# A strided 1-D convolution with norm and GELU, forward and backward: paired sums joined, and pair sums of four combinations kept off the raw step buffers

## The chip, the cores and the metric

The kernel runs on one core of a Trainium2 chip. The metric is device time in microseconds (us) of one launch, inputs and outputs in device memory. A core has a matrix engine (TensorE, PE in the profile, with PEld for its weight loads), a vector engine (VectorE, DVE), a scalar engine (ScalarE, ACT), GpSimd (POOL), and SyncE (SP), whose queue issues the DMA transfers here. Each engine takes its own instructions in their order; semaphores tie the engines together.

## The reference

A convolution of 31 taps and stride 2 over 2 x 16000 steps of 256 channels, a normalisation over time per channel, GELU, and the gradients of all four inputs.

```python
def _fwd_reference(x, w, gn_gamma, gn_beta):
    B, T, D = x.shape            # 2, 16000, 256
    K = w.shape[0]               # 31
    s = 2
    L = (T - K) // s + 1         # 7985
    h = jnp.einsum('blc,cd->bld', x[:, 0:s * L:s, :], w[0])
    for i in range(1, K):
        h = h + jnp.einsum('blc,cd->bld', x[:, i:i + s * L:s, :], w[i])
    mu = jnp.einsum('bld->bd', h)[:, None, :] / L
    var = jnp.einsum('bld->bd', (h - mu) ** 2)[:, None, :] / L
    h = (h - mu) / jnp.sqrt(var + 1e-5)
    h = h * gn_gamma[None, None, :] + gn_beta[None, None, :]
    return _gelu(h)

def reference(x, w, gn_gamma, gn_beta, grad_out):
    out, vjp = jax.vjp(_fwd_reference, x, w, gn_gamma, gn_beta)
    return (out, *vjp(grad_out))
```

## The kernel before

**Stages.** F0 and F1 are the forward convolution of the two batches, in four chunks each (`forward`); G0 and G1 the gradient with respect to x (`input_grad`); W the gradient of the weights (`weight_grad`). Normalisation and GELU (`gelu_batch`) of a batch run beside the stage that follows its convolution.

**Fewer products, more sums.** A convolution over an index of two values is computed with three products in place of four: one with the first operand (called `A`), one with the second (`C_`), and one with a sum or difference (`B_`). This is done on several index levels, so that matmuls are traded for sums of bf16 data on DVE. In the forward stages `f_sums` makes them: `first` level sums for a branch, `second` (for the leaves `A` and `C_`) and `third`, each over `F = 1088` columns and, as a rule, for both parities of a step. The sums for parity 0 take `o[:, 0]` and `o[:, 1]` in place; those for parity 1 take `o[:, 1]` and `o[:, 0]` one column on. So they are two instructions, of 1088 and 1087 columns (the helper `tt`, L561). In the input gradient `g_sums` does the same with 258 and 257 columns for two channel halves (L1121). `f_three_ac` and `g_three_ac` use the two halves of a `third` sum in separate groups of matmuls, `f_three_b` and `f_outer` the product with weight differences (`w_sub`, L551), whose results ACT copies with both signs.

**The weight gradient.** `weight_grad` goes through nine combinations n = 0 to 8 of two indices, in the order `COMBOS`: (A,A), (A,C_), (A,B_), (C_,B_), (B_,B_), (B_,A), (B_,C_), (C_,A), (C_,C_). Each needs four tiles of x (`x_tile`, one for each of two batches and two values of a third index) and two of gradient differences (`d_tile`). A tile of x is one raw load for n = 0, 1, 7, 8; two raw loads that DVE adds (`w_add`, L1413) for n = 3, 5, 6; and for n = 2 and 4 a sum of tiles that are there. The second raw load of a tile goes to one of two buffers `XR`, at bytes 57344 and 65536 of the arena. In each combination DVE makes pair sums of x (`pair_x`, L1508) and pair differences of the gradient (`pair_d`, L1516, two instructions of 1024 elements, one for each of two places around a middle one); PE makes their products (`w_pairs`, `w_single`), `w_both` (L1540) puts two partial results into one accumulator, and `leaf_d` (L1587) makes differences along the last index. `pair_x` and `pair_d` write to a set of buffers that `place(n)` picks in turn from those that n allows: "all" is always there, "early" for n below 2, and "late", which starts at byte 57344 and so lies on both `XR`, for all n but 3 and 5. After combination 3, `w_done` spills four partial results (`pcd`) to memory, and combination 7 loads them back.

**The order of the instructions** isn't that of the program. `Plan` collects every operation with its engine, an estimated duration and the cells of memory that it touches. `Plan.order` gives each a due time from what needs it, from `slack` and a table `lead` (an offset for each kind of operation and stage), and `Plan.listing` then lists the operations engine by engine, the earliest due first among those ready; `look` is how far PE may reach ahead, `pads` what is allowed for around a DMA, `PACE` how the GELU units are spread over a stage, and `plan.hold` keeps what was recorded under it back until PE has come so far. The program is emitted in that order, so that each engine's queue is fixed at build time. `w2_part` prepares transposed weights for the input gradient, a quarter in each chunk of F0.

## Time and profile before

| | us |
|---|---|
| median of 3 runs | 1187.01 |
| lowest and highest | 1183.07 and 1188.23 |
| the profiled execution, its own time | 1189.54 |
| its span | 1187.8 |
| PE busy | 1149.0 |
| DVE busy | 1047.6 |
| ACT busy | 570.0 |

The profile is one execution. The page gives for each engine the busy time, its share of the span and the number of instructions; the stretches give the busy time of each engine in a window, with the clock granted to TensorE (1.00 is full) and the mean busy share of the DMA engines; the groups give a line, engine, operation, shapes and count, then busy time, mean ns of one instruction, idle time ahead of them and what ended it. Rows in order of time begin with the start and the length in us, and end with the idle time ahead of them and its releaser in brackets. By the rows of PE, the forward stages end near 428 us, the input gradient near 861 us, and the weight gradient takes the rest.

### The profile page before, as it was taken

The page shows a single profiled execution, that of the slowest core. Times are in us where ns is not written, and L with a number is a line of the kernel's source. Part 1 is how long each engine was busy: PE and PEld are TensorE (multiplying, and loading weights), DVE is VectorE, ACT ScalarE, POOL GpSimd, SP SyncE. Part 2 cuts the span into 40 slices and gives each one's busy share as a digit, 9 for nine tenths or more (in the row PEclk, how much of TensorE's full clock was granted, in tenths as well). Part 3 has the DMA queues.
Part 4 walks back from the last instruction along what each step waited for, and adds up shares of the span by engine and source line. Part 5 has one row for each costly group of instructions (what it writes and reads, how often), then busy time and mean ns, then how long its engine had stood idle before and what let it go on. Part 6 is the DMA issues. An engine that isn't in the chain of part 4 may idle for free.

```text
span 1187.8 us, 19338 instructions
## 1 busy us (share of the span) xinstructions
PE 1149.0 (97%) x7739; PEld 763.5 (64%) x7796; DVE 1047.6 (88%) x1358; ACT 570.0 (48%) x873; POOL 18.9 (2%) x67
## 2 busy tenths in 40 slices
PE   5999999999999999999999999999999999989998
PEld 3888889777777964444444444444488656656685
DVE  7997898799999989999879997788889898777995
ACT  1254454788885578978884476433322212111200
POOL 0000000000000000000000000000000000000000
PEclk9999999999999999999999999999999999999999
DMA  9446949968986799567639998697998824986774
GB/s 212 73 115 122 200 121 182 205 146 204 204 209 124 270 353 252 167 225 186 221 115 292 270 329 265 161 318 266 317 235 266 271 90 151 359 300 198 239 219 140
DMA packets 334100, 255.17 MB, mean 215 GB/s; under 512 B 187500, under 2 KB 312682, under 8 KB 325738
## 3 DMA queue, kind: packets, MB, share of 16 engines
q1 hardware_dynamic: 333818, 253.93, 76.6%
q8 instruction: 61, 1.00, 0.3%
q14 instruction: 29, 0.24, 0.1%
q0 software_dynamic: 192, 0.00, 0.0%
HBM read 118.95 MB, written 89.62 MB: 176 GB/s over the span
## 4 chain that ended last, share of the span: by engine, by line
PE 46%; DVE 14%; DMA 6%; issue 4%; ACT 1%; SPq 0%; DVEq 0%; ACTq 0%
PE ps L1162 27%; PE ps L1447 15%; PE ps L596 4%; DVE arena L1413 3%; DMA arena<-in_x_dram 2%; DMA arena<-dnd 2%; DVE arena L1357 2%; DVE arena L1587 2%; DVE ps L676 1%; DVE arena L676 1%; DVE arena L1516 1%; DVE arena L1508 1%; DMA dnd<-arena 1%; DVE arena L1121 1%; DVE ps L1540 1%
## 5 line engine op out<-in xcount | busy, mean ns | idle before, releaser
L1162 PE MATMUL ps<-arena 128*128 128x512 bf16 x1974 | 429.7, 376 | 6.6 <-DVE ps L676 3.6
L596 PE MATMUL ps<-arena 128*128 128x256 bf16 (+4 forms) x3460 | 408.2, 281 | 17.8 <-DVE arena L551 7.1
L596 PEld LDWEIGHTS <-arena 128*128 128x128 bf16 x3460 | 338.1, 99 | 87.7 <-DVE arena L551 7.5
L1162 PEld LDWEIGHTS <-arena 128*128 128x128 bf16 x2016 | 197.3, 98 | 237.7 <-issue 6.8
L1447 PE MATMUL ps<-arena 128*128 128x256 bf16 (+1 forms) x2305 | 312.1, 298 | 10.5 <-DVE arena L1508 7.3
L1447 PEld LDWEIGHTS <-arena 128*128 128x128 bf16 x2320 | 228.1, 98 | 94.6 <-DVE arena L1508 8.7
L691 ACT ACTIVATE arena<-ps 128x1024 f32<-128x1024 f32 (+1 forms) x143 | 145.7, 1020 | 285.3 <-PE ps L1447 98.1
L561 DVE TENSOR_TENSOR arena<-arena 128x1087 bf16<-128x1087 bf16 (+3 forms) x211 | 175.5, 866 | 13.7 <-PE ps L596 12.4
L968 DVE TENSOR_TENSOR arena<-arena 128x1024 bf16<-128x1024 bf16 x160 | 107.0, 683 | 8.5 <-ACT arena L962 3.9
L1413 DVE TENSOR_TENSOR arena<-arena 128x4096 bf16<-128x4096 bf16 x38 | 86.3, 2284 | 20.8 <-DMA arena<-in_x_dram 19.5
L1121 DVE TENSOR_TENSOR arena<-arena 128x516 bf16<-128x516 bf16 (+3 forms) x176 | 83.6, 506 | 8.6 <-PE ps L1162 8.0
L676 DVE TENSOR_TENSOR ps<-ps,arena 128x1024 f32<-128x1024 f32 x60 | 73.1, 1224 | 7.9 <-PE ps L1447 4.5
L1357 DVE TENSOR_TENSOR arena<-arena 128x768 bf16<-128x768 bf16 (+3 forms) x112 | 65.4, 636 | 9.9 <-DMA arena<-dnd 4.7
L711 ACT ACTIVATE arena<-ps 128x512 bf16<-128x512 f32 (+1 forms) x64 | 36.9, 578 | 70.4 <-PE ps L596 67.9
L676 DVE TENSOR_TENSOR ps<-arena,ps 128x1024 f32<-128x1024 f32 x44 | 53.8, 1223 | 9.3 <-PE ps L1162 5.5
L1532 ACT COPY ps<-ps 128x256 f32<-128x256 f32 x54 | 19.3, 357 | 78.7 <-PE ps L1447 77.6
L1587 DVE TENSOR_TENSOR arena<-arena 128x2304 bf16<-128x2304 bf16 x36 | 47.4, 1348 | 4.8 <-PE ps L1447 4.8
L1516 DVE TENSOR_TENSOR arena<-arena 128x1024 bf16<-128x1024 bf16 x76 | 48.7, 682 | 1.6 <-DMA arena<-d2d 1.6
L551 DVE TENSOR_TENSOR arena<-arena 128x2048 bf16<-128x2048 bf16 (+1 forms) x52 | 49.8, 989 | 0.0
L958 DVE SCALAR_TENSOR_TENSOR arena<-arena 128x1024 bf16<-128x1024 bf16 x32 | 39.0, 1219 | 11.3 <-ACT arena L956 11.1
L1189 ACT ACTIVATE ps<-ps 128x512 f32<-128x512 f32 x48 | 27.9, 582 | 41.1 <-PE ps L1162 38.0
L1508 DVE TENSOR_TENSOR arena<-arena 128x2048 bf16<-128x2048 bf16 x38 | 45.3, 1216 | 1.2 <-PE ps L1162 1.2
(79 smaller groups left out, 632.8 us busy)
## 6 DMA issues: line engine op xcount, KB each, us to landing
arena<-in_x_dram SPq DMA_DIRECT2D x40, 1024.0 KB, 9.8
arena<-d2d SPq DMA_DIRECT2D x16, 1216.0 KB, 11.5
out_dram<-arena SPq DMA_DIRECT2D x14, 1024.0 KB, 4.4
d2d<-arena SPq DMA_DIRECT2D x30, 384.0 KB, 7.1
arena<-dnd SPq DMA_DIRECT2D x10, 960.0 KB, 5.8
vl<-arena SPq DMA_DIRECT2D x36, 256.0 KB, 3.3
arena<-vl SPq DMA_DIRECT2D x9, 1024.0 KB, 6.8
hd<-arena SPq DMA_DIRECT2D x8, 1024.0 KB, 5.0
```

What stands on the lines that cost most here:

```text
L561: lambda: nc.vector.tensor_tensor(out=o, in0=a, in1=b, op=ALU.add))
L596: yield nc.tensor.matmul(ps[:, dh, cs], lhsT=wt, rhs=mv, start=s0, stop=False, skip_group_check=True)
L676: add("DVE", dve(1024, 1), [out], [a, b], lambda: nc.vector.tensor_tensor(out=out, in0=a, in1=b, op=op))
L691: lambda: nc.scalar.activation(out=out, in_=ps, func=ACT.Copy, scale=scale))
L968: add("DVE", dve(1024), [o], [a, b_], lambda: V.tensor_tensor(out=o, in0=a, in1=b_, op=op))
L1121: lambda: nc.vector.tensor_tensor(out=o, in0=a, in1=b, op=ALU.add))
L1162: yield nc.tensor.matmul(ps[:, e, 0:wide], lhsT=lt, rhs=mv, start=s0, stop=False, skip_group_check=True)
L1357: lambda: nc.vector.tensor_tensor(out=out, in0=a, in1=b_, op=ALU.subtract))
L1413: add("DVE", dve(4096), [o], [a, b], lambda: nc.vector.tensor_tensor(out=o, in0=a, in1=b, op=ALU.add))
L1447: yield nc.tensor.matmul(ps[:, s, c0:c1], lhsT=lt, rhs=mv, start=s0, stop=False, skip_group_check=True)
L1516: add("DVE", dve(1024), [d4[:, j]], [d], lambda j=j, o=o, st_=st_: nc.vector.tensor_tensor(out=d4[:, j], in0=d[:, o:o + 3 * st_ + 1:st_, : ...
L1587: add("DVE", dve(2304), [DL[i3, b]], [D2[b]], lambda b=b, i3=i3, o_=o_: nc.vector.tensor_tensor(out=DL[i3, b], in0=D2[b][:, o_:o_ + 17:2, ...
```

## The change

It has four parts.

1. Sums that came in twos become one instruction. `crossed(v, n)` makes the second operand: it starts at row 1 of v, and its second row is row 0, one column on, so that the step between the rows is 1 - k, backwards. It is used in `f_sums` (`first` of C_, `second` of C_, `third`), in `g_sums` (the same three) and, written out, in `pair_d`, whose first operand steps back by k rows and whose second repeats a row block with a step of 0. The third buffers `U` become one tile of two rows for it, and the last column of both rows is set to zero at the start.
2. `place(n)` no longer offers "late" for n = 2 and 4, as it did not for 3 and 5.
3. In `f_first` the weight differences are recorded in another order around the first sums, and `w_sub` can be made to follow a tile. `w2_part` of the last chunk is recorded one branch earlier.
4. The planner's numbers change: `slack`, `look`, `pads`, `PACE`, and the whole table `lead`. With that, the order of the instructions changes on PE, DVE, ACT and SP in all stages. The number of PE's, ACT's and SP's instructions stays.

```diff
-        self.slack = 70.0
+        self.slack = 50.0
-        self.look = 13
-        self.pads = (3122.5, 3149.5, 2842.0)
+        self.look = 14
+        self.pads = (3356.0, 3383.0, 3083.0)
         self.lead = {
...
-    U = [(sb(o, F), sb(o + 2176, F)) for o in (138240, 142592, 205312)]
+    U = [sb(o, 2, F) for o in (138240, 142592, 205312)]
...
-    def w_sub(o, a, b):
+    def w_sub(o, a, b, *then):
         n = o.free_size()
-        add("DVE", dve(n), [o], [a, b], lambda: nc.vector.tensor_tensor(out=o, in0=a, in1=b, op=ALU.subtract))
+        add("DVE", dve(n), [o], [a, b, *then], lambda: nc.vector.tensor_tensor(out=o, in0=a, in1=b, op=ALU.subtract))
...
-                tt(E1[:, 0], xt[:, 0, 3], xt[:, 1, 0])
-                tt(E1[:, 1, 0:F - 1], xt[:, 1, 3, 0:F - 1], xt[:, 0, 0, 1:F])
+                tt(E1[:, :, 0:F - 1], xt[:, :, 3, 0:F - 1], crossed(xt[:, :, 0], F - 1))
...
-            tt(u[0], o[:, 0], o[:, 1], behind)
-            tt(u[1][:, 0:F - 1], o[:, 1, 0:F - 1], o[:, 0, 1:F], behind)
+            tt(u[:, :, 0:F - 1], o[:, :, 0:F - 1], crossed(o, F - 1), behind)
...
-                tt(lc[:, 0], E1[:, 0], E0[:, 1], behind)
-                tt(lc[:, 1, 0:F - 1], E1[:, 1, 0:F - 1], E0[:, 0, 1:F], behind)
+                tt(lc[:, :, 0:F - 1], E1[:, :, 0:F - 1], crossed(E0, F - 1), behind)
...
+    def crossed(v, n):
+
+        a = v[..., 1, 0:n]
+        dims = [list(x) for x in a.ap]
+        k = [list(x) for x in v.ap][-2][0]
+        return bass.AP(tensor=a.tensor, offset=a.offset, ap=dims[:-1] + [[1 - k, 2], [1, n]])
...
     def f_first(xt):
-        for sl in (A, C_):
-            for ch in range(2):
-                for v in ([slice(None)] if ch or sl == C_ else [0, 1]):
-                    w_sub(*(W[br][:, sl, ch, :, v] for br in (B_, C_, A)))
         ops, third, second = f_sums(xt, 0, 0, B_, 0, [W[B_][:, A, 0, :, v] for v in range(2)])
+        w_sub(*(W[br][:, A, 0, :, 0] for br in (B_, C_, A)))
         second(A)
+        w_sub(*(W[br][:, A, 0, :, 1] for br in (B_, C_, A)), ops[A])
+        w_sub(*(W[br][:, A, 1] for br in (B_, C_, A)))
+        for ch in range(2):
+            w_sub(*(W[br][:, C_, ch] for br in (B_, C_, A)))
         second(C_)
...
-                tt(sc[:, :, 1, 0, 0:n], et[:, :, 3, 0, 0:n], et[:, :, 0, 1, 0:n])
-                tt(sc[:, :, 1, 1, 0:n - 1], et[:, :, 3, 1, 0:n - 1], et[:, :, 0, 0, 1:n])
+                tt(sc[:, :, 1, :, 0:n], et[:, :, 3, :, 0:n], crossed(et[:, :, 0], n))
...
-            tt(u[:, 0, :, 0:n], e[:, :, 0, 0:n], e[:, :, 1, 0:n])
-            tt(u[:, 1, :, 0:n - 1], e[:, :, 1, 0:n - 1], e[:, :, 0, 1:n])
+            tt(u.rearrange("p j d f -> p d j f")[:, :, :, 0:n - 1], e[:, :, :, 0:n - 1], crossed(e, n - 1))
...
-                tt(l[:, 1, :, 0, 0:n], e1[:, :, 0, 0:n], e0[:, :, 1, 0:n])
-                tt(l[:, 1, :, 1, 0:n - 1], e1[:, :, 1, 0:n - 1], e0[:, :, 0, 1:n])
+                tt(l[:, 1, :, :, 0:n], e1[:, :, :, 0:n], crossed(e0, n))
...
-        for j, o in ((0, o0), (1, o1)):
-            st_ = abs(o0 - o1)
-            add("DVE", dve(1024), [d4[:, j]], [d], lambda j=j, o=o, st_=st_: nc.vector.tensor_tensor(
-                out=d4[:, j], in0=d[:, o:o + 3 * st_ + 1:st_, :], in1=d[:, om:om + 3 * st_ + 1:st_, :], op=ALU.subtract))
+        k = abs(o0 - o1)
+        a, m = d[:, o0], d[:, om]
+        a = bass.AP(tensor=a.tensor, offset=a.offset, ap=[list(a.ap[0]), [-k * D, 2], [k * D, 4], [1, D]])
+        m = bass.AP(tensor=m.tensor, offset=m.offset, ap=[list(m.ap[0]), [0, 2], [k * D, 4], [1, D]])
+        add("DVE", dve(2048), [d4], [d], lambda: nc.vector.tensor_tensor(out=d4, in0=a, in1=m, op=ALU.subtract))
...
-            ks = ("all",) + (("early",) if n < 2 else ()) + (("late",) if n not in (3, 5) else ())
+            ks = ("all",) + (("early",) if n < 2 else ()) + (("late",) if n not in (2, 3, 4, 5) else ())
...
-    PACE = ((1385.0, 117.0), (191.0, 24.5))
+    PACE = ((1423.0, 75.5), (75.0, 11.0))
...
-        if b == 0 and br == C_:
+        if b == 0:
             plan.hold = plan.npe
-            w2_part(c)
+            if br == (A if c == 3 else C_):
+                w2_part(c)
             plan.hold = -1
```

More of the change, by code (lines that the diff above doesn't have):

```diff
@@ L48, in __init__ @@
         self.pe = 0.0
-        self.slack = 70.0
+        self.slack = 50.0
         self.hold = -1
-        self.look = 13
-        self.pads = (3122.5, 3149.5, 2842.0)
+        self.look = 14
+        self.pads = (3356.0, 3383.0, 3083.0)
         self.lead = {
-            "F0 f_mm f_three_ac": -2.5,
-            "F0 f_mm f_three_b": -4.0,
-            "F0 f_mm pe_turn": 9.5,
-            "F0 f_three_b f_first": 2.0,
-            "F0 f_three_b forward": 2.5,
-            "F0 keep f_first": 4.5,
-            "F0 load load_w": -4.5,
-            "F0 put x_first": -4.5,
-            "F0 tt second": -1.0,
-            "F0 tt third": -1.5,
-            "F0 turn w2_part": 8.0,
-            "F0 turn x_load": -3.5,
-            "F0 ve f_first": -1.0,
-            "F0 ve f_seed": -4.0,
-            "F0 w_sub f_first": 2.0,
-            "F1 f_mm f_leaf": -4.0,
-            "F1 f_mm f_three_ac": -3.0,
-            "F1 f_mm f_three_b": -9.5,
-            "F1 f_three_b forward": 4.5,
-            "F1 gelu_unit gelu_batch": 3.0,
-            "F1 load gelu_unit": -2.0,
-            "F1 tiny elem_finalize": 2.0,
-            "F1 tiny fwd_stats": -11.5,
-            "F1 tt f_sums": 1.5,
-            "F1 tt gelu_unit": -4.0,
-            "F1 tt second": -7.5,
-            "F1 turn x_load": -3.0,
-            "G0 e_comp conv_stem_kernel": -1.0,
-            "G0 g_mm g_three_ac": 3.0,
-            "G0 g_mm g_three_b": -3.0,
-            "G0 g_three_b input_grad": 6.0,
-            "G0 keep g_evac": -3.0,
-            "G0 load dn_turn": 1.0,
-            "G0 load e_load": 4.5,
-            "G0 load gelu_unit": 2.0,
-            "G0 load load_w2": 4.0,
-            "G0 tiny elem_finalize": -8.5,
-            "G0 tt first": -2.0,
-            "G0 tt second": -9.0,
-            "G0 turn gelu_batch": -7.0,
-            "G0 w_sub load_w2": -8.0,
-            "G1 e_comp conv_stem_kernel": 12.5,
-            "G1 g_mm g_leaf": -4.0,
-            "G1 g_mm g_outer": -1.5,
-            "G1 g_mm g_three_ac": -4.0,
-            "G1 keep g_evac": -10.5,
-            "G1 load dn_turn": -11.5,
-            "G1 load e_load": -2.5,
-            "G1 load g_evac": 20.0,
-            "G1 signed g_seed": -7.5,
-            "G1 spread e_comp": -5.5,
-            "G1 sub d2_piece": -7.5,
-            "G1 tt first": 9.5,
-            "G1 tt second": -5.5,
-            "G1 tt third": -2.0,
-            "G1 ve_neg g_seed": 11.5,
-            "W keep w_keep": -2.0,
-            "W keep weight_grad": 3.0,
-            "W leaf_d weight_grad": -2.0,
-            "W pair_x weight_grad": -1.5,
-            "W turn out0_late": -7.0,
-            "W ve w_done": 12.0,
-            "W ve weight_grad": -3.5,
-            "W w_add weight_grad": -2.0,
-            "W w_add x_tile": 3.0,
-            "W w_both weight_grad": 9.0,
-            "W w_emit w_done": 7.5,
-            "W w_mm w_leaf": -3.5,
-            "W w_mm w_single": 0.5,
-            "W w_pairs weight_grad": -2.5,
@@ new lines, in __init__ @@
+            "F0 f_evac last": -6.0,
+            "F0 f_mm pe_turn": -9.5,
+            "F0 f_outer forward": 3.5,
+            "F0 load put": 5.0,
+            "F0 put x_first": 5.0,
+            "F0 tt second": 11.0,
+            "F0 tt third": 1.5,
+            "F0 turn x_load": -6.0,
+            "F0 ve f_first": 1.5,
+            "F0 ve f_seed": -3.0,
+            "F0 w_sub f_first": 3.5,
+            "F0 w_sub w2_part": -6.0,
+            "F1 f_evac last": -4.0,
+            "F1 f_mm f_leaf": -6.5,
@@ new lines, in __init__ @@
+            "F1 f_mm f_three_ac": -7.0,
+            "F1 f_mm f_three_b": -8.0,
+            "F1 f_outer forward": -8.0,
+            "F1 f_three_b forward": 8.5,
+            "F1 gelu_unit gelu_batch": 1.5,
+            "F1 keep f_evac": 1.5,
+            "F1 load f_evac": -1.5,
+            "F1 load gelu_unit": -0.5,
+            "F1 tt f_sums": -4.5,
+            "F1 tt gelu_unit": 0.5,
+            "F1 tt third": 0.5,
+            "F1 turn gelu_unit": -2.0,
+            "F1 ve f_seed": 4.0,
@@ new lines, in __init__ @@
+            "F1 zero f_evac": 6.0,
+            "G0 e_comp conv_stem_kernel": -5.0,
+            "G0 g_mm g_three_ac": 2.0,
+            "G0 g_mm g_three_b": 1.5,
+            "G0 g_three_b input_grad": -8.0,
+            "G0 gelu_batch conv_stem_kernel": 0.5,
+            "G0 keep g_evac": -4.0,
+            "G0 keep g_seed": 1.5,
+            "G0 load g_evac": 5.5,
+            "G0 load gelu_unit": -2.0,
+            "G0 spread e_comp": 4.0,
+            "G0 tiny elem_finalize": -10.0,
+            "G0 tiny fwd_stats": -4.5,
@@ new lines, in __init__ @@
+            "G0 tt first": -2.5,
+            "G0 turn dn_turn": 6.0,
+            "G0 turn gelu_batch": -8.0,
+            "G0 ve g_seed": -8.0,
+            "G0 ve_neg g_seed": 4.0,
+            "G0 zero gelu_batch": 6.0,
+            "G1 e_comp conv_stem_kernel": 4.0,
+            "G1 g_mm g_leaf": -5.0,
+            "G1 g_mm g_three_ac": -2.5,
+            "G1 g_mm g_three_b": 3.0,
+            "G1 half_neg signed": -10.0,
+            "G1 keep g_evac": -5.0,
+            "G1 load dn_turn": 2.5,
@@ new lines, in __init__ @@
+            "G1 load e_load": -2.5,
+            "G1 load g_evac": 13.0,
+            "G1 signed g_seed": -6.5,
+            "G1 sub d2_piece": -4.5,
+            "G1 tt second": -3.5,
+            "G1 turn dn_turn": 1.0,
+            "G1 ve g_seed": 4.0,
+            "G1 w_sub w2_outer": -14.5,
+            "W keep w_keep": -7.5,
+            "W leaf_d weight_grad": -6.5,
+            "W load out0_late": -4.0,
+            "W load w_emit": 0.5,
+            "W load x_raw": 2.0,
+            "W pair_x weight_grad": -1.0,
@@ L124, in __init__ @@
+            "W ve weight_grad": 10.0,
+            "W w_add weight_grad": -1.0,
+            "W w_add x_tile": -1.5,
+            "W w_both weight_grad": 4.5,
+            "W w_emit w_done": 7.0,
+            "W w_emit weight_grad": 8.0,
+            "W w_mm w_leaf": 4.5,
+            "W w_mm w_pairs": 0.5,
+            "W w_mm w_single": -0.5,
         }
@@ L474, in conv_stem_kernel @@
     add("POOL", 0.4, [zt2[:]], [], lambda: nc.gpsimd.memset(zt2[:], 0.0))
-    for t, n in ((S[C_][:, 1, 1, F - 1:F], 1), (LL[0][1][:, 1, F - 1:F], 1), (LL[1][1][:, 1, F - 1:F], 1),
-                 *((u[1][:, F - 1:F], 1) for u in U)):
+    for t, n in ((S[C_][:, :, 1, F - 1:F], 2), (LL[0][1][:, :, F - 1:F], 2), (LL[1][1][:, :, F - 1:F], 2),
+                 *((u[:, :, F - 1:F], 2) for u in U)):
         zero(t, n, "DVE")
@@ L634, in f_three_ac @@
     def f_three_ac(ps, br, lf, u, co, we, wo):
-        for half, ua, ww in ((0, u[0], we), (1, u[1], wo)):
+        for half, ua, ww in ((0, u[:, 0], we), (1, u[:, 1], wo)):
             for dh in range(2):
@@ L811, in f_again @@
     def f_again():
-        zero(U[2][1][:, F - 1:F], 1, "DVE")
+        zero(U[2][:, :, F - 1:F], 2, "DVE")
         for br in FLAST:
```

## The prediction

> **What bounds the kernel now.** I read the page's totals first, then the busy time by stretches, then what TensorE waits for.

> ```profile
> span 1187.8 us, 19338 instructions
> PE 1149.0 (97%) x7739; PEld 763.5 (64%) x7796; DVE 1047.6 (88%) x1358; ACT 570.0 (48%) x873; POOL 18.9 (2%) x67
> ```

> TensorE (PE) is busy for 1149.0 of 1187.8 us, so 38.8 us of idle time is all that a change outside the matmuls can win, and the matmuls stay the same. VectorE (DVE) has 88%, but it counts only where PE waits for it. Stretches (columns: length, busy time of PE, PEld, DVE, ACT, POOL, granted clock, DMA share, GB/s):

> ```profile
> 0.00:30.00 30.00, 17.05 (x116) 11.64 (x117) 22.89 (x34) 5.04 (x9) 1.55 (x9) 0.94 0.96 210
> 30.00:60.00 30.00, 30.00 (x276) 26.75 (x275) 29.96 (x32) 8.60 (x18) 0.00 (x0) 1.00 0.49 77
> ...
> 960.00:1060.00 100.00, 91.66 (x642) 64.33 (x644) 81.44 (x65) 18.72 (x30) 0.00 (x0) 0.97 0.76 251
> ...
> 1130.00:1188.00 58.00, 53.34 (x424) 41.39 (x424) 44.80 (x43) 2.14 (x6) 0.53 (x1) 1.00 0.60 175
> ```

> The start holds 12.95 us of PE idle, the end 4.66 us (the last stores, mostly), and one stretch in the weight gradient 8.34 us, at a clock of 0.97. The remaining 12.85 us are spread over the other thousand. What PE waits for:

> ```profile
> PE ps L1447 <- DVE arena L1508: 7.3, 5, 4.2
> PE ps L596 <- DVE arena L551: 7.1, 2, 4.0
> ...
> PE ps L1162 <- DVE ps L676: 3.6, 5, 1.3
> PE ps L596 <- ACT arena L711: 2.3, 4, 0.8
> ...
> PE ps L596 <- DVE arena L561: 1.2, 1, 1.2
> ```

> The pair sums of the weight gradient (L1508) are the largest releaser; the weight differences of the start (L551) come next. The convolution's own step sums (L561) held PE once, those of the input gradient (L1121) never. So the change has to be priced mainly in 960 to 1060, and only secondly by the DVE time that it saves.

> **The joined sums.** DVE's groups by shape:

> ```profile
> L561 DVE TENSOR_TENSOR arena<-arena 128x1088 bf16<-128x1088 bf16 x87 | 61.8, 717 | 7.9 <-PE ps L596 7.1 <-ACT arena L511 0.7
> L561 DVE TENSOR_TENSOR arena<-arena 128x1087 bf16<-128x1087 bf16 x85 | 60.7, 720 | 5.6 <-PE ps L596 5.3
> ...
> L1516 DVE TENSOR_TENSOR arena<-arena 128x1024 bf16<-128x1024 bf16 x76 | 48.7, 682 | 1.6 <-DMA arena<-d2d 1.6
> ...
> L1508 DVE TENSOR_TENSOR arena<-arena 128x2048 bf16<-128x2048 bf16 x38 | 45.3, 1216 | 1.2 <-PE ps L1162 1.2
> L561 DVE TENSOR_TENSOR arena<-arena 128x2176 bf16<-128x2176 bf16 x31 | 39.8, 1283 | 0.2
> ...
> L1121 DVE TENSOR_TENSOR arena<-arena 128x514 bf16<-128x514 bf16 x68 | 28.1, 422 | 0.9 <-PE ps L1162 0.9
> ...
> L676 DVE TENSOR_TENSOR arena<-arena 128x1024 f32<-128x1024 f32 x20 | 24.1, 1220 | 8.2 <-ACT arena L666 6.7 <-ACT arena L691 1.4
> ...
> L1121 DVE TENSOR_TENSOR arena<-arena 128x1036 bf16<-128x1036 bf16 x32 | 22.1, 690 | 2.1 <-PE ps L1162 1.6
> ```

> The 85 sums of 1087 elements each lose their partner of 1088, the 68 of 514 theirs of 516, and the 76 differences at L1516 become 38: 85 + 68 + 38 = 191 instructions go. A joined one should take what the same size takes now: 1283 ns for 2174 elements, 690 for 1028 to 1032, 1216 for 2048. By these means each join saves some 150 ns, but neighbours overlap, so I take the step from start to start:

> ```profile
> 16.88 13.71 DVE L551 TENSOR_TENSOR arena<-arena 128x2048 bf16<-128x2048 bf16 x12
> 365.65 4.29 DVE L968 TENSOR_TENSOR arena<-arena 128x1024 bf16<-128x1024 bf16 x7
> ```

> (13.71 - 1.21) / 11 = 1.136 us for 2048 elements, (4.29 - 0.68) / 6 = 0.602 us for 1024: a join saves 2 x 0.602 - 1.136 = 0.068 us, and 191 save 13.0 us of DVE's 1047.6. On the path that sets the end lies little of it. In the start three joins stand ahead of the weight differences that PE waits for: 0.2 us. Elsewhere the 12.85 us of small waits are the most that a less loaded DVE could win, and as every instruction is ordered anew by the planner they could as well grow; I take 0, with 12.85 us less as one bound and, for the other, the slower rival below.

> No operand with a backward step over rows is in the trace. From below, the row of 2176 (1283 ns); from above, the rate of the 1024 fp32 sums (1220 ns, so 1.045 ns per element behind 150 ns fixed, against 0.52). I take the lower: each row of the crosswise operand is a forward run, and the sums of 1087 elements already read a run that begins one element in, at 720 ns. [...]

> **The raw step buffers.** Before, combination 4 (the fifth, both indices B_) keeps its first pair sums in the "late" set, which lies on the two buffers into which the raw steps of combination 5 are loaded. After, only the "all" set is left to it. For combinations 2, 3 and 5 the rotation gave "all" before too, so that combination 4 alone changes. What this costs now (DVE, then PE, then the queue of SP, then ACT):

> ```profile
> 992.43 2.35 DVE L1508 TENSOR_TENSOR arena<-arena 128x2048 bf16<-128x2048 bf16 x2
> ...
> 995.91 2.35 DVE L1508 TENSOR_TENSOR arena<-arena 128x2048 bf16<-128x2048 bf16 x2
> ...
> 1015.12 2.29 DVE L1413 TENSOR_TENSOR arena<-arena 128x4096 bf16<-128x4096 bf16 x1 [9.38 <-DMA arena<-in_x_dram]
> 1017.33 2.35 DVE L1540 TENSOR_TENSOR ps<-ps,arena 128x1024 f32<-128x1024 f32 x2
> ```

> ```profile
> 974.40 0.61 PE L1447 MATMUL ps<-arena 128*128 128x256 bf16 x4 [1.72 <-DVE arena L1508]
> ...
> 1018.61 21.40 PE L1447 MATMUL ps<-arena 128*128 128x256 bf16 x130 [1.66 <-DVE ps L1540]
> 1044.18 53.48 PE L1447 MATMUL ps<-arena 128*128 128x256 bf16 x344 [4.17 <-DVE arena L1508]
> ```

> ```profile
> 991.77 5.58 SPq L415 DMA_DIRECT2D arena<-in_x_dram  x3
> ...
> 1006.50 1.26 SPq L415 DMA_DIRECT2D arena<-in_x_dram  x2
> ```

> ```profile
> 1006.50 1.13 ACT L1532 COPY ps<-ps 128x256 f32<-128x256 f32 x3 [0.56 <-PE ps L1447]
> ```

> The pair sums of combination 4 are written at 992.43; PE ends its pass over them at 1006.50, where ACT begins to copy the result; the first load into a raw buffer is issued at that moment. It lands some 9 us later, DVE stands 9.38 us in L1413, the seed sum L1540 is queued behind it and PE loses 1.66 us; the last additions of combination 5 then come late and PE loses 4.17 us at 1044. After, SP issues two raw loads for combination 5 ahead of combination 4's gradient differences, and all eight ahead of the four spills that they stood between. The DMA engines have room for that:

> ```profile
> 980.00:990.00 10.00, 9.95 (x77) 7.42 (x77) 9.95 (x9) 1.02 (x1) 0.00 (x0) 1.00 0.00 0
> ...
> 1020.00:1030.00 10.00, 9.95 (x73) 7.05 (x73) 6.95 (x6) 2.05 (x2) 0.00 (x0) 1.00 1.04 401
> ```

> They do nothing from 980 to 990 and are full at 1020. With both waits the slow clock goes that follows them:

> ```profile
> 976.00:978.00 2.00, 2.00 (x12) 1.41 (x10) 2.00 (x2) 0.00 (x0) 0.00 (x0) 0.50 1.14 344
> 978.00:980.00 2.00, 2.00 (x14) 1.48 (x13) 2.00 (x3) 1.02 (x1) 0.00 (x0) 0.64 0.15 44
> ...
> 1044.00:1046.00 2.00, 1.82 (x9) 1.29 (x10) 1.42 (x2) 0.00 (x0) 0.00 (x0) 0.57 1.07 359
> 1046.00:1048.00 2.00, 2.00 (x13) 1.44 (x11) 1.32 (x2) 0.99 (x3) 0.00 (x0) 0.58 1.09 357
> ```

> Behind 1044 that is 2 x (0.43 + 0.42) = 1.7 us lost. So 1.66 + 4.17 + 1.7 = 7.5 us go. Against it stands a new wait: combination 4's second pair sums (now at 995.91) share their place with the first and wait until 1006.50, 10.6 us later, with an addition of raw steps, the pair differences and L1540 queued behind them. DVE stood idle there anyway, and PE has the single products to do, from 1006.50 to 1016.9; I charge 0.5 us (bounds 0 and the 1.66 us that L1540 costs now). Net: -7.0 us.

> At 974.40, in combination 3, PE waits 1.72 us for pair sums that stand in DVE's queue behind additions and differences, and a clock of 0.50 and 0.64 follows: 2 x (0.50 + 0.36) = 1.7 us. In the new order fewer of these stand between the first and the second pair sums (one difference and four evictions). I count half of 3.4 us: -1.7 us, bounds 0 and 3.4. [...]

> Sum: -0.2 - 7.0 - 1.7 = -8.9 us against this execution, whose own time is 1189.54 us for a span of 1187.8; the median of the runs is 1187.01. A difference carries over: 1187.0 - 8.9 = 1178.1 us. Its own range, from the bounds of the three terms (-0.2, -5.9 to -7.5, 0 to -3.4) and some 2 us of the new order either way: 1174 to 1183.

> **The rivals.**
> - The wait moves. Combination 6 needs eight more raw loads through the same two buffers, and the DMA share is already 1.04 there. If those are then late as these were, 5.8 us of waits come back and only the clock and the small terms stay: about 1185 us. Against it: they too start earlier.
> - Slower, by joining. A joined sum gives its first half only when both are done, 0.6 us later. The 89 sums whose halves go to separate groups of matmuls decide: it costs from the point at which PE arrives within 0.6 us of them. DVE has no slack from 30 to 60 (29.96 of 30). If a third of them is met so, 30 x 0.6 = 18 us: 1196 us. Against it: one wait for L561 in the whole trace.
> - The operand is slow. (1.045 - 0.52) x (85 x 2174 + 68 x 1030 + 38 x 2048) = 175 us more on DVE, 1209 us busy; with its idle 7.1 us at the start and 13.2 us at the end about 1230 us. The 720 ns speak against it. [...]
> - More is won: half of the 12.85 us of small waits goes as well, 1171 us.

> **How the numbers follow.** Forecast 0.53, wait moved 0.24, slower by joining 0.10, slow operand 0.04, more won 0.09. Range 1168 to 1196: from the better case to the slower one, without the slow operand. Half a per cent (5.9 us) is about what a measurement of this kernel can tell from no change: faster is below 1181.1. Of the forecast 0.46 lies there, with the better case 0.55; the rest and the moved wait are 0.31; slower 0.14.

> **What would show it.** Right: 191 fewer DVE instructions, joined means near 1283, 690 and 1216 ns, DVE busy near 1035 us; in combination 4 no L1413 wait of 9 us and no PE wait above 1 us for pair sums before combination 5; clock 1.00 throughout 980 to 1060. Wrong: joined means near 2400 ns; PE waits for L561's or L1121's successors in many places; the wait for raw loads one combination later; or new idle time before 860, which would be the new order and no term of mine.

## The result, and the profile after

| | us | ratio to before, 95% interval |
|---|---|---|
| before, 8 runs beside the changed kernel | 1185.65 | |
| after, 8 runs | 1192.12 (1189.97 to 1196.12) | 1.0054 [1.0038, 1.0071] |
| forecast | 1178.1 (1168 to 1196) | |

The change made the kernel slower by 0.54%, where 0.75% faster was forecast. The profiled execution of after took 1192.77 us by its own time, near the median; that of before took 1189.54, more than any of its eight runs. So the two profiles differ by 3.2 us where the medians differ by 6.5, and what follows splits the 3.2. The page's totals of after (busy time, share of the span, instructions):

```profile
span 1191.0 us, 19174 instructions
PE 1151.9 (97%) x7796; PEld 763.1 (64%) x7796; DVE 1034.4 (87%) x1167; ACT 570.9 (48%) x873; POOL 21.2 (2%) x67
```

DVE has 191 instructions and 13.2 us less, as forecast. The groups of the joined sums, by shape (busy us, mean ns, then the idle time ahead of them):

```profile
L567 DVE TENSOR_TENSOR arena<-arena 128x2174 bf16<-128x2174 bf16 x85 | 108.1, 1288 | 18.4 <-PE ps L599 16.5 <-DMA arena<-in_x_dram 1.7
...
L1526 DVE TENSOR_TENSOR arena<-arena 128x2048 bf16<-128x2048 bf16 x38 | 45.1, 1216 | 1.4 <-PE ps L1455 1.4
L1132 DVE TENSOR_TENSOR arena<-arena 128x1028 bf16<-128x1028 bf16 x36 | 24.8, 692 | 4.6 <-PE ps L1170 2.6 <-ACT arena L1092 2.0
```

Forecast were 1283, 1216 and 690 ns: with the backward step the means are 5, 0 and 2 ns above that. So far all is as foretold. Where PE's stages begin tells what isn't. The rows are PE's timeline, first of before, then of after; L1162 and L1170 are the input gradient, L1447 and L1455 the weight gradient:

```profile
428.89 3.40 PE L1162 MATMUL ps<-arena 128*128 128x512 bf16 x15
...
861.19 3.98 PE L1447 MATMUL ps<-arena 128*128 128x256 bf16 x35
...
1161.10 22.71 PE L1447 MATMUL ps<-arena 128*128 128x512 bf16 x142 [0.36 <-DVE ps L676]
```

```profile
438.69 11.61 PE L1170 MATMUL ps<-arena 128*128 128x512 bf16 x54
...
875.56 285.95 PE L1455 MATMUL ps<-arena 128*128 128x256 bf16 x2176
1161.77 22.71 PE L1455 MATMUL ps<-arena 128*128 128x512 bf16 x144 [0.26 <-DVE ps L686]
```

From these rows and the two spans:

| part | before | after | difference |
|---|---|---|---|
| forward, to the input gradient's solid run | 428.9 | 438.7 | +9.8 |
| input gradient | 432.3 | 436.9 | +4.6 |
| weight gradient, to the last matmul's end | 322.6 | 308.9 | -13.7 |
| after the last matmul | 4.0 | 6.5 | +2.5 |
| span | 1187.8 | 1191.0 | +3.2 |

The weight gradient won 13.7 us, more than the 8.7 forecast for it: after 875.56 PE runs 285.95 us without one wait. 16.9 us were lost elsewhere, 14.4 of them before 876. PE's groups say in which waits, before, then after (busy us, mean ns, idle time ahead and what ended most of it):

```profile
L1162 PE MATMUL ps<-arena 128*128 128x512 bf16 x1974 | 429.7, 376 | 6.6 <-DVE ps L676 3.6
L596 PE MATMUL ps<-arena 128*128 128x256 bf16 (+4 forms) x3460 | 408.2, 281 | 17.8 <-DVE arena L551 7.1
L1447 PE MATMUL ps<-arena 128*128 128x256 bf16 (+1 forms) x2305 | 312.1, 298 | 10.5 <-DVE arena L1508 7.3
```

```profile
L1170 PE MATMUL ps<-arena 128*128 128x512 bf16 (+1 forms) x2016 | 433.5, 377 | 7.3 <-DVE ps L686 2.7
L599 PE MATMUL ps<-arena 128*128 128x256 bf16 (+4 forms) x3460 | 410.8, 282 | 24.8 <-DVE arena L557 7.6
L1455 PE MATMUL ps<-arena 128*128 128x256 bf16 (+1 forms) x2320 | 308.6, 296 | 0.4 <-DVE ps L686 0.3
```

The forward stages (L596, now L599) idle 7.0 us more. From 347.52 a stretch of 3.41 us has a granted clock of 0.50, and before has none there: another 1.7 us, by an estimate of half its length. Some 1 us of the +9.8 is not placed. In the input gradient PE's named waits grow from 4.4 us (L676 3.6, L691 0.8; the other 2.2 of the 6.6 have no releaser, in a trace that lacks 42 of 2016 matmul records) to 7.3, and 3.41 us at a clock of 0.50 from 722.99 cost 1.7 more by the same estimate: that is its +4.6. PE's waits in after (us in total, times, longest):

```profile
PE ps L599 <- DVE arena L557: 7.6, 3, 3.9
PE ps L599 <- ACT arena L721: 7.3, 7, 2.7
...
PE ps L1170 <- ACT arena L1092: 2.2, 1, 2.2
PE ps L599 <- ACT arena L701: 2.2, 1, 2.2
PE ps L1170 <- ACT ps L1197: 2.1, 1, 2.1
PE ps L599 <- DVE arena L567: 1.0, 2, 0.7
```

New are the waits for ACT: 9.5 us for the copies of the convolution's accumulators (L721 in `f_evac`, L701 in `keep`), which took 2.3 us before, and 4.3 us in the input gradient, at 652 and 722 us (L1092 `spread`, L1197 in `g_three_b`). None is named by the change. The joined sums (L567) held PE for 1.0 us in all. The longest of the ACT waits, in ACT's timeline of after, then PE's:

```profile
365.74 0.60 ACT L721 ACTIVATE arena<-ps 128x512 bf16<-128x512 f32 x1 [2.65 <-PE ps L599]
...
366.33 1.23 ACT L965 ACTIVATE arena<-arena,stats 128x1024 bf16<-128x1024 bf16 x1
367.46 1.23 ACT L967 ACTIVATE arena<-arena,stats 128x1024 bf16<-128x1024 bf16 x1
368.59 0.58 ACT L721 ACTIVATE arena<-ps 128x512 bf16<-128x512 f32 x1
```

```profile
347.31 19.27 PE L599 MATMUL ps<-arena 128*128 128x256 bf16 x128 [2.19 <-ACT arena L701]
369.31 56.72 PE L599 MATMUL ps<-arena 128*128 128x256 bf16 x496 [2.74 <-ACT arena L721]
```

PE ends at 347.31 + 19.27 = 366.58. The first half of its accumulator is copied at once; the second half stands behind two GELU activations (L965, L967) of the other batch and is copied at 368.59. PE has nothing else to do in its order, and waits 2.74 us.

### The profile page after: what moved, and what is told of

Same layout as the page of the kernel before. It is cut to its first block, busy times and chain, and to the rows that moved or that the text cites. A ratio compares the mean times of both kernels' runs of the same rounds, so it can differ in the third digit from the quotient of the medians.

```text
span 1191.0 us, 19174 instructions
## 1 busy us (share of the span) xinstructions
PE 1151.9 (97%) x7796; PEld 763.1 (64%) x7796; DVE 1034.4 (87%) x1167; ACT 570.9 (48%) x873; POOL 21.2 (2%) x67
## 4 chain that ended last, share of the span: by engine, by line
PE 49%; DVE 5%; issue 4%; DMA 1%; ACT 1%; SPq 0%; POOL 0%; DVEq 0%; POOLq 0%; ACTq 0%
PE ps L1170 27%; PE ps L1455 22%; DVE arena L1132 1%; DMA arena<-dnd 1%; DVE arena L1365 1%; DVE arena L1526 1%; DMA out_dram<-arena 1%; DVE ps L686 1%; DVE arena L1596 0%; DVE arena L1484 0%; DVE arena L1516 0%; SPq L421 0%; DVE ps L1549 0%; DVE arena L1073 0%; DVE arena L686 0%
## 5 line engine op out<-in xcount | busy, mean ns | idle before, releaser
L1170 PE MATMUL ps<-arena 128*128 128x512 bf16 (+1 forms) x2016 | 433.5, 377 | 7.3 <-DVE ps L686 2.7
L599 PE MATMUL ps<-arena 128*128 128x256 bf16 (+4 forms) x3460 | 410.8, 282 | 24.8 <-DVE arena L557 7.6
L599 PEld LDWEIGHTS <-arena 128*128 128x128 bf16 x3460 | 338.6, 99 | 97.0 <-issue 12.1
L1170 PEld LDWEIGHTS <-arena 128*128 128x128 bf16 x2016 | 197.7, 98 | 242.0 <-issue 12.1
L1455 PE MATMUL ps<-arena 128*128 128x256 bf16 (+1 forms) x2320 | 308.6, 296 | 0.4 <-DVE ps L686 0.3
L701 ACT ACTIVATE arena<-ps 128x1024 f32<-128x1024 f32 (+1 forms) x143 | 145.8, 1021 | 296.6 <-PE ps L1170 100.4
L1455 PEld LDWEIGHTS <-arena 128*128 128x128 bf16 x2320 | 226.9, 98 | 82.1 <-issue 0.7
L567 DVE TENSOR_TENSOR arena<-arena 128x2174 bf16<-128x2174 bf16 (+3 forms) x126 | 166.5, 1350 | 20.7 <-PE ps L599 18.0
L979 DVE TENSOR_TENSOR arena<-arena 128x1024 bf16<-128x1024 bf16 x160 | 107.7, 686 | 15.1 <-ACT arena L971 8.9
L1421 DVE TENSOR_TENSOR arena<-arena 128x4096 bf16<-128x4096 bf16 x38 | 85.8, 2284 | 10.8 <-DMA arena<-in_x_dram 5.5
L1132 DVE TENSOR_TENSOR arena<-arena 128x1036 bf16<-128x1036 bf16 (+3 forms) x108 | 76.4, 731 | 13.3 <-PE ps L1170 10.9
L721 ACT ACTIVATE arena<-ps 128x512 bf16<-128x512 f32 (+1 forms) x64 | 37.0, 581 | 78.8 <-PE ps L599 75.8
L969 DVE SCALAR_TENSOR_TENSOR arena<-arena 128x1024 bf16<-128x1024 bf16 x32 | 39.1, 1221 | 13.9 <-ACT arena L967 13.7
L1541 ACT COPY ps<-ps 128x256 f32<-128x256 f32 x54 | 19.3, 358 | 66.1 <-PE ps L1455 65.0
L1516 DVE TENSOR_TENSOR arena<-arena 128x2048 bf16<-128x2048 bf16 x38 | 44.9, 1216 | 4.2 <-PE ps L1170 3.4
L1526 DVE TENSOR_TENSOR arena<-arena 128x2048 bf16<-128x2048 bf16 x38 | 45.1, 1216 | 1.4 <-PE ps L1455 1.4
L1197 ACT ACTIVATE ps<-ps 128x512 f32<-128x512 f32 x48 | 28.0, 584 | 37.2 <-PE ps L1170 37.1
```

What stands on the lines that cost most here:

```text
L567: lambda: nc.vector.tensor_tensor(out=o, in0=a, in1=b, op=ALU.add))
L599: yield nc.tensor.matmul(ps[:, dh, cs], lhsT=wt, rhs=mv, start=s0, stop=False, skip_group_check=True)
L701: lambda: nc.scalar.activation(out=out, in_=ps, func=ACT.Copy, scale=scale))
L979: add("DVE", dve(1024), [o], [a, b_], lambda: V.tensor_tensor(out=o, in0=a, in1=b_, op=op))
L1132: lambda: nc.vector.tensor_tensor(out=o, in0=a, in1=b, op=ALU.add))
L1170: yield nc.tensor.matmul(ps[:, e, 0:wide], lhsT=lt, rhs=mv, start=s0, stop=False, skip_group_check=True)
```

## The experiments

Two theories were open. *Order*: the new numbers and the new set of operations make the planner list all queues anew, and the lists it finds lose 16 us; buffers and joins are as forecast. *Joins*: the joined sums themselves lose it, since their first halves come 0.6 us later. Each ratio below is to runs of before taken beside that kernel. "Joined at the old place" below means that the second half's place in DVE's queue takes the joined sum, and the first half's is left empty.

**The change of place alone** (label e1_place_only), on the kernel before; the order differs from before in the weight gradient only.

```diff
-            ks = ("all",) + (("early",) if n < 2 else ()) + (("late",) if n not in (3, 5) else ())
+            ks = ("all",) + (("early",) if n < 2 else ()) + (("late",) if n not in (2, 3, 4, 5) else ())
```

> Before with one line changed: pair sums of combinations 2 to 5 kept off the raw step buffers; the order of the instructions then differs from before only inside the weight gradient. Theory (the buffers were worth what was forecast, and the loss lies elsewhere): the waits of 1.7 us and 4.2 us in the weight gradient and the slow clock behind them go, 5 to 8 us less than before, about 1179 us. Rival (the weight gradient of the changed kernel is free of waits only through the new planner's numbers): 0 to 2 us less than before, about 1185 us.

1179.82 us beside 1187.11: 0.9934 [0.9913, 0.9955]. PE's timeline in the weight gradient of this run:

```profile
973.08 114.72 PE L1447 MATMUL ps<-arena 128*128 128x256 bf16 x784 [2.36 <-DVE arena L1508]
...
1151.24 22.71 PE L1447 MATMUL ps<-arena 128*128 128x512 bf16 x144 [0.36 <-DVE ps L676]
```

From 973.08 on PE runs 114.72 us through: the waits at 1018.61 and 1044.18 are gone. The wait in combination 3 stays (2.36 us). One line of the diff gives 7.3 us.

**The joins alone, with before's order** (e5_join_same_order): 178 of the 191 pairs are joined at the old place; PE, ACT, POOL and SP keep before's order. The other 13 have a reader of the first half between the two and stay apart, so that this run doesn't test them.

```diff
...
+        for i, j, fn in self.twins:
+            e, l = (i, j) if at[i] < at[j] else (j, i)
+            if any(e in self.ops[order[k]]["preds"] for k in range(at[e] + 1, at[l])):
+                continue
+            self.ops[e]["fn"], self.ops[l]["fn"] = None, fn
...
```

> Before with 178 of its 191 twins of sums joined, and the order of all other instructions left exactly as before (a joined sum stands at the place of its second twin; 13 twins with an instruction between them that needs the first stay apart). Theory C (a joined sum costs nothing by itself, what costs is the order that the planner makes around it): 1182 to 1187 us, 0 to 4 us less than before. Rival B (the first half comes later and TensorE waits for it): 1190 us or more, with new waits for L567-like sums in the forward stages and the input gradient.

1187.8 us beside 1187.12: 1.0007 [0.9994, 1.002]. The page of this run:

```profile
PE 1147.8 (97%) x7739; PEld 762.5 (64%) x7796; DVE 1038.4 (87%) x1180; ACT 570.3 (48%) x873; POOL 20.4 (2%) x67
```

DVE is 9.2 us less busy than before, and the time is the same. It lies 0.8 us above the range expected without a price and below the 1190 expected with one.

**Joins and place, with e1's order** (e6_join_place): both edits above, with 180 pairs joined.

> The same joining (180 of 191) on top of the kernel with the buffer change alone, whose order it keeps. Theory C: 1175 to 1180 us, faster than both kernels. Rival B: 1183 us or more.

1180.08 us: 0.9939 [0.9921, 0.9957]. That is e1's ratio: with the place changed the joins give nothing and cost nothing either.

**After, unjoined** (e7_after_unjoined): the kernel after, in which each joined sum is issued as two; the order is after's on every engine.

```diff
...
+    def halves(op, *parts):
+        def go():
+            for o, a, b in parts:
+                yield nc.vector.tensor_tensor(out=o, in0=a, in1=b, op=op)
+        return go
...
```

> After with each joined sum issued again as two instructions at its place; the order of all other instructions stays exactly that of after. Theory C: not faster than after, 1191 to 1198 us, since DVE has 13 us more to do and the waits come from the order. Rival B: 1182 to 1189 us, because the first halves come earlier again.

1196.08 us: 1.0071 [1.005, 1.0091]. The loss stays with the first halves of all 191 pairs early again, so the theory of the joins falls. Beside e1 this kernel has the same instructions on each engine, 1358 on DVE; only their order differs, and the few lines of `f_first` and `w2_part` that belong to it. 1.0071 against 0.9934 is 1.4%, or some 16 us, for order alone.

**The planner's numbers.** Three runs: after with all numbers of before (e2_old_numbers); before with all numbers of after (e3_new_numbers); before with the joins, planned anew with before's numbers (e4_joins_only). The first edit is, in part:

```diff
-        self.slack = 50.0
+        self.slack = 70.0
-        self.look = 14
-        self.pads = (3356.0, 3383.0, 3083.0)
+        self.look = 13
+        self.pads = (3122.5, 3149.5, 2842.0)
         self.lead = {
...
```

> After with the planner's numbers of before (slack, look, pads, lead, PACE); joined sums, buffer change and the new order of recording stay. Theory A (the new numbers cause the new idle time of the forward stages, where evacuations stand behind GELU work in ScalarE's queue): TensorE's idle time up to 425 us falls from 24.8 to about 18 us, the weight gradient keeps most of its win, 1172 to 1180 us. Rival B (the joined sums cause it, by giving their first half later): the new idle time stays, 1187 to 1193 us.

> Before with the planner's numbers of after and nothing else. Theory A: the forward stages lose 7 to 10 us as in the changed kernel, and without joined sums DVE is fuller, so it is slower than after: 1192 to 1200 us. Rival B: the forward stages stay as before, 1183 to 1188 us.

> Before with the joined sums alone, at the planner's numbers, buffers and order of recording of before. Theory A: 1180 to 1187 us, the 13 us of DVE time lie off the path. Rival B: TensorE waits more often for DVE's sums in the forward stages, 1192 to 1197 us.

| | us | ratio | PE idle: forward, input gradient, weight gradient |
|---|---|---|---|
| e2, after's operations, before's numbers | 1196.48 | 1.0079 [1.0054, 1.0105] | 21.0, 12.8, 2.3 |
| e3, before's operations, after's numbers | 1231.57 | 1.0387 [1.036, 1.0413] | 25.7, 19.7, 14.7 |
| e4, before's operations joined, before's numbers | 1215.42 | 1.0244 [1.0214, 1.0273] | 19.1, 19.7, 10.1 |

All three lie above every range that was expected of them. So "the new numbers are worse" isn't right either: with the old ones the changed kernel is no faster (1.0079 against 1.0054). Each of these lists, made with the numbers of one kernel and the operations of another, loses 0.8 to 3.9% against before; that numbers fit one set of operations only is the likely reading, and wasn't tried by itself. The joins, planned anew, cost 2.4% in e4 and nothing in e5: the price is the list's, not the instructions'.

**After, with the forward leads of before** (e8_after_f_before): the entries of F0 and F1 in `lead`, and the first pair of `PACE`.

```diff
...
-    PACE = ((1423.0, 75.5), (75.0, 11.0))
+    PACE = ((1385.0, 117.0), (75.0, 11.0))
...
```

> After with the planner's leads of the stages F0 and F1 and the first PACE pair of before; slack, look, pads and the numbers of the other stages stay those of after. If the new leads and pace of the forward stages put the evacuations behind GELU work: TensorE's idle time up to 425 us falls from 24.8 towards 18 us, 1182 to 1187 us. If it is the interplay of all numbers with the joined durations: no gain, 1189 to 1200 us.

1192.51 us: 1.0048 [1.0033, 1.0062]. PE's groups of this run:

```profile
L1169 PE MATMUL ps<-arena 128*128 128x512 bf16 (+1 forms) x1974 | 431.4, 377 | 16.0 <-DVE ps L685 6.0 <-DVE ps L689 3.3 <-ACT arena L700 2.6
L598 PE MATMUL ps<-arena 128*128 128x256 bf16 (+4 forms) x3460 | 409.2, 281 | 18.5 <-DVE arena L556 6.2 <-DMA arena<-in_x_dram 5.4 <-ACT arena L720 2.6
```

The forward waits for ACT went (2.6 us for the evacuations) and 6.3 us of forward idle time with them, but the input gradient idles 16.0 us in place of 7.3. The forward gain is given back one stage later.

**Evacuations ahead of GELU in ACT's queue.** In e9_evac_first the convolution's evacuations are put ahead of GELU activations that stand right before them, where the plan has them ready; in e10_evac_first_all those of the input gradient too; e11_place_evac_first does it to e1. All other queues stay.

```diff
...
+            while q > 0 and p - q < 4 and "gelu" in ops[act[q - 1]]["kind"] and act[q - 1] not in ops[i]["preds"] \
+                    and at <= self.start[act[q - 1]] + 1.0:
+                q -= 1
+            if q < p:
+                act.insert(q, act.pop(p))
...
```

> The kernel after, in which only ACT's queue is changed: each evacuation of a convolution accumulator (the copies of f_evac and keep) that stood right behind GELU activations is put ahead of up to four of them, where by the plan its accumulator is ready no later than 1 us after the passed activation would start. The order of PE, DVE, POOL and SP stays. If the 9.5 us that PE waits for L721 and L701 in the second forward stage come from the place of the evacuations in ACT's queue, these waits fall below 4 us. If this time is then kept, the kernel takes 1185 to 1188 us; if the input gradient gives it back, as it gave back the forward gain with the forward leads of before, 1191 to 1193 us, with the weight gradient starting at about 874 us again. If the waits stay, the evacuations were late for their accumulators and not for their place.

> As the run before, and the copies that PE waits for in the input gradient (spread, and the sign copy of g_three_b) are put ahead of GELU activations in the same way. If the place in ACT's queue is what holds the second input gradient, its waits for L1092 and L1197 (4.3 us together) go too, the weight gradient starts some 4 to 12 us earlier than at 875.6 and the time is 1179 to 1187 us. If what holds it is the late gradient of the second batch (its loads and VectorE's work on them), the waits move to other releasers and the time stays at 1190 to 1193 us.

> The kernel before with the change of place alone, and with the same rule on ACT's queue as in the run before this one. If evacuations behind GELU activations cost time in any order of this kernel, it takes 1176 to 1179 us against the 1179.8 us of the change of place alone. If the order of before had no such loss to give (its waits for evacuations are 2.3 us in sum), it stays within 1179 to 1182 us.

| | us | ratio |
|---|---|---|
| e9, after, forward | 1199.08 | 1.0101 [1.0082, 1.012] |
| e10, after, forward and input gradient | 1197.43 | 1.009 [1.0071, 1.0108] |
| e11, on e1 | 1183.12 | 0.9971 [0.9959, 0.9982] |

All three are slower than the kernel that they start from, and above every range that was expected of them. In e9 the waits for evacuations stay (6.6 + 3.6 us), so nothing was won; at the place of 366 us the rule left two GELU activations between the halves. What was lost shows on DVE near 260 us. After first, then e9 (lines 32 higher), each DVE and PE; L969 and L1001 are the GELU step that needs ACT's L967 and L999:

```profile
260.44 1.22 DVE L969 SCALAR_TENSOR_TENSOR arena<-arena 128x1024 bf16<-128x1024 bf16 x1
...
262.18 2.41 DVE L567 TENSOR_TENSOR arena<-arena 128x4352 bf16<-128x4352 bf16 x1
```

```profile
264.65 5.53 PE L599 MATMUL ps<-arena 128*128 128x256 bf16 x45 [0.68 <-DVE arena L567]
```

```profile
262.89 1.23 DVE L1001 SCALAR_TENSOR_TENSOR arena<-arena 128x1024 bf16<-128x1024 bf16 x1 [1.36 <-ACT arena L999]
...
264.63 2.42 DVE L599 TENSOR_TENSOR arena<-arena 128x4352 bf16<-128x4352 bf16 x1
```

```profile
267.11 3.21 PE L631 MATMUL ps<-arena 128*128 128x256 bf16 x20 [3.02 <-DVE arena L599]
```

ACT's GELU activation comes later, DVE's next GELU step waits for it, the sum of 4352 elements is queued behind that step and starts 2.45 us later, and PE waits 3.02 us in place of 0.68. In e10 the waits for L1092 and L1197 stay too (2.2 and 2.3 us); the rows of after show why. PE, then ACT:

```profile
652.26 26.06 PE L1170 MATMUL ps<-arena 128*128 128x512 bf16 x120 [2.23 <-ACT arena L1092]
...
722.72 22.57 PE L1170 MATMUL ps<-arena 128*128 128x512 bf16 x97 [2.11 <-ACT ps L1197]
```

```profile
720.56 0.62 ACT L1092 COPY arena<-arena 128x512 bf16<-128x512 bf16 x1 [1.08 <-POOL arena L1109]
...
721.57 0.61 ACT L1092 COPY arena<-arena 128x512 bf16<-128x512 bf16 x1
722.08 0.59 ACT L1197 ACTIVATE ps<-ps 128x512 f32<-128x512 f32 x1
```

The sign copy L1197 stands behind copies of `spread`, which wait for POOL, and not behind GELU: the second batch's gradient is being prepared there, and the rule has nothing to move.

**The halves together** (e12_halves_together): in after, the second half's evacuation is put right behind the first where up to four GELU activations stand between. ACT's queue differs at some 40 of its 740 places; the order of DVE's operations in the two traces is the same.

```diff
...
+            while q > 0 and p - q < 4 and "gelu" in ops[act[q - 1]]["kind"]:
+                q -= 1
+            if q < p and q > 0 and "f_evac" in ops[act[q - 1]]["kind"]:
+                act.insert(q, act.pop(p))
...
```

> The kernel after, in which only ACT's queue is changed, and less than in the two runs that moved evacuations ahead of GELU activations: where the second half of a convolution accumulator's evacuation stands up to four GELU activations behind the first half, it is put right behind the first half. Each passed activation moves by 0.6 us. At 365.74 us in the profile of after two activations (2.4 us) stand between the halves, and PE waits 2.74 us. If such places are what the second forward stage loses, PE's waits for L721 fall from 7.3 us to about 4 us (0.8 us each is left at the places where nothing stands between) and the forward stages end 2 to 3 us earlier; if nothing else is disturbed the kernel takes 1188 to 1190 us. If VectorE's queue holds it again, because its GELU steps now wait for ACT with pair sums behind them (1.36 us at 262.9 us in the run e9_evac_first, where the next pair sums then came 3.0 us late for PE), the time stays at 1191 us or rises.

1212.24 us: 1.0225 [1.0209, 1.024], the strongest effect of an edit that touches neither the work nor DVE's order. The expectation allowed a rise and gave it no size; 20 us were not foreseen. ACT, DVE and PE of this run (lines 30 higher than after's):

```profile
267.26 0.60 ACT L751 ACTIVATE arena<-ps 128x512 bf16<-128x512 f32 x1 [2.63 <-PE ps L629]
...
267.85 0.59 ACT L751 ACTIVATE arena<-ps 128x512 bf16<-128x512 f32 x1
...
268.42 1.24 ACT L997 ACTIVATE arena<-arena,stats 128x1024 bf16<-128x1024 bf16 x1
```

```profile
269.69 1.22 DVE L999 SCALAR_TENSOR_TENSOR arena<-arena 128x1024 bf16<-128x1024 bf16 x1 [4.70 <-ACT arena L997]
...
271.43 2.42 DVE L597 TENSOR_TENSOR arena<-arena 128x4352 bf16<-128x4352 bf16 x1
```

```profile
273.90 2.32 PE L629 MATMUL ps<-arena 128*128 128x256 bf16 x10 [5.80 <-DVE arena L597]
```

Now GELU stands behind evacuations that wait for PE, DVE stands 4.70 us, and PE 5.80 us, for the same sum. The wait is a ring: PE needs DVE's sum, which is queued behind a GELU step, which needs ACT, which stands behind an evacuation, which needs PE's matmuls. Over the whole run DVE's GELU step waits 21.9 us for ACT against 13.7 in after (after first):

```profile
L969 DVE SCALAR_TENSOR_TENSOR arena<-arena 128x1024 bf16<-128x1024 bf16 x32 | 39.1, 1221 | 13.9 <-ACT arena L967 13.7
...
L999 DVE SCALAR_TENSOR_TENSOR arena<-arena 128x1024 bf16<-128x1024 bf16 x32 | 39.0, 1219 | 23.1 <-ACT arena L997 21.9 <-ACT arena L995 1.1
```

## Why the prediction was wrong

**The raw step buffers: right.** -7.0 was forecast for combination 4, and e1, which does this alone, is 7.3 us faster. In after the first raw load of combination 5 is issued at 997.62 (SP's timeline) and three more from 1010.64, all ahead of 1015.01, where ACT begins the copies (L1541) that stood at 1006.50 before, behind PE's pass over combination 4:

```profile
997.62 16.29 SPq L421 DMA_DIRECT2D arena<-in_x_dram  x4
```

`w_add` (L1421) waits no longer than 3.18 us between 985 and 1075, where it stood 9.38. The new wait for combination 4's second pair sums, charged 0.5 us, cost PE nothing. The rival "the wait moves" fell: no wait came back in combination 6.

**Combination 3: undersized.** -1.7 was forecast from the new order. The weight gradient as a whole won 13.7 us, 8.5 of it by the place alone (e1's weight gradient runs from 859.80 to its last matmul's end at 1173.95, 314.1 us against 322.6), so that the order gave some 5 there, above the bound of 3.4. It took the whole 3.4 us of combination 3, where half was counted, and some 2 us of smaller waits: behind 875.56 none is left before the last 23 us.

**The joined sums: right.** Means and DVE's saving came as forecast, and "little of it lies on the path" was right: e5 measures 0.07% with an interval of 0.13% to either side. Of the -0.2 us for the start nothing is left: PE's long run begins at 22.24 in place of 22.69, and new waits of 0.53 and 0.27 us follow it. The rival "slower by joining" had the direction but not the mechanism: e5, e6 and e7 show no price of the later first half, and PE waits 1.0 us for L567 in all. The slow operand fell (1288 ns).

**The step that failed: "as every instruction is ordered anew by the planner they could as well grow; I take 0, with 12.85 us less as one bound".** This term was +16.9 us before and behind the weight gradient's matmuls, less 5 in it, +12 net. The prediction had named the sign itself, new idle time before 860, and had given it no price. Three faults are in it. The bound on the bad side was borrowed from the rival of the joins, whose mechanism has nothing to do with it, and the forecast's own range allowed 2 us either way. The reading of waits as "12.85 us of small waits" took them for noise around a mean, as likely to shrink as to grow. Every list that was made anew for the whole kernel came out slower than before's: after by 0.54%, e2, e3, e4 and e8 by 0.5 to 3.9%. So before's list was a good one for its operations, and a new one was more likely to lose. And the built order was there to be read: that evacuations stood behind two GELU activations in ACT's queue was fixed before the run.

Two smaller figures of the prediction don't come out of its own terms: the range begins at 1168, where the better case gives 1171 and 12.85 us less would give 1165; and some of the 12.85 us may be no wait at all (2.2 us in the input gradient have no releaser, as said above).

**Where the order loses,** by what is shown: in the second forward stage evacuations stand behind GELU activations (2.74 us at 366, PE's releaser and ACT's queue agree); in the input gradient PE waits for `spread` and for what is queued with it at 652 and 722; behind the last matmul it takes 2.5 us more (6.5 us; 6.3 to 8.2 in e2, e3, e4, e7 and e8, and 3.9 to 4.0 in before, e1, e5 and e6). What isn't shown is a cure: e8 moved the loss a stage on, e9 and e12 moved the copies and lost more to DVE's queue. That the input gradient is bound by how early the second batch's gradient is ready is argued from e8 and e10, and was not tried by itself. Part 3 of the change wasn't either; e4 lost without it.

**A version that beats both** is the smallest one: e1, one line of the diff, at 0.9934 of before, and with the joins e6 at 0.9939, no better.

## What to carry to other kernels

When a change makes a planner list the queues anew, that is an edit of its own, and here it was the largest: price it apart, by building the new operations in the old order (e5, e6) and the old operations in the new one (e7), before the operations are credited or blamed. A saving on an engine where PE does not wait for it was worth nothing here (9.2 us of DVE busy time, a ratio of 1.0007), while one instruction's place in a queue was worth microseconds (in after PE waited 2.74 us at 366 for a copy behind two GELU activations). Before moving an instruction ahead in one queue, ask which queue's head waits for the one that is passed.

## What the runs showed of the hardware

DVE took a second operand whose row step is negative, and in `pair_d` one with a step of 0 as well, at the rate of plain rows: 1288 ns for 2174 elements beside 1283 for 2176, and in `pair_d` 1216 for 2048 beside 1216 for the pair sums of before. The second crosswise row starts one element in; the 1288 ns include it.

ACT and DVE took the instructions of the rows above in the order of their queues: in e12 DVE's sum at 271.43 began only behind the GELU step that had stood 4.70 us, and in after ACT's copy at 368.59 only behind two GELU activations of 1.23 us each. Moved copies made 8.2 us more of DVE's waits for ACT at the GELU step in e12 (21.9 us against 13.7).

```profile
344.11:347.52 3.41, 1.22 (x12) 0.94 (x10) 3.41 (x5) 3.41 (x4) 0.96 (x1) 1.00 0.33 75
347.52:350.93 3.41, 3.41 (x19) 2.34 (x17) 3.41 (x6) 3.04 (x5) 0.00 (x0) 0.50 1.21 289
364.59:368.00 3.41, 1.99 (x18) 1.46 (x15) 1.49 (x3) 2.26 (x4) 0.51 (x1) 1.00 0.55 145
368.00:371.41 3.41, 2.10 (x21) 2.01 (x22) 2.66 (x3) 1.47 (x4) 0.00 (x0) 1.00 0.00 0
371.41:374.82 3.41, 3.41 (x30) 2.66 (x28) 1.94 (x3) 3.38 (x6) 0.00 (x0) 1.00 0.03 7
```

The shorter wait fell into one step, which held 2.19 us of idle time, and a step at 0.50 followed. The longer one was split over two, which held 1.42 and 1.31 us, and none followed. The two traces have 677 such steps at full clock from 16.87 us (before) and 16.43 us (after) to the last matmul. Six were followed by a step at 0.50: they held 2.41, 2.25 and 3.31 us of PE idle time in before (from 20.28, 972.60 and 1040.87) and 2.40, 2.19 and 2.11 in after (from 19.84, 344.11 and 719.58). Of the others none held more than 1.64 us (from 16.87 in before).
